# Two layers of channel mixing by 15 products from the third batch element on, their results in banks of two PSUM pools in turn

## The chip, the cores and the metric

The kernel runs on one core of a Trainium2 chip. The metric is the device time of one execution in microseconds. TensorE (PE) multiplies; its weight loads are listed as PEld. VectorE (DVE), ScalarE (ACT) and GpSimd (POOL) do the element work, SyncE (SP) issues most DMAs. Each engine works through its own queue in order. Matmul results stand in PSUM banks, everything else in SBUF.

## The reference

All tensors are float32. The batch has 8 elements b, S = 448 positions, 12 heads of 64, so C = 768 channels.

```python
q_n, k_n = rmsnorm(q, g_q), rmsnorm(k, g_k)
scores = (q_n @ k_n.T) / 8
attn = softmax(scores) ;  x = (attn @ v)            # (8, 448, 768), heads side by side
h = relu(x.T @ w_tok1) @ w_tok2                      # (768 x 448) (448 x 256) (256 x 448)
u = x + h.T
out = u + relu(u @ w_ch1) @ w_ch2                    # 768 -> 1536 -> 768
```

The last line is the channel mixing, two layers of matrix products. The change concerns these.

## The kernel before

**Elements in a pipeline.** PE works in the order in which the program issues its instructions. `middle_items(b)` gives the work of element b as a list of small items: token mixing (`tok1`, `tok2`), then `ch1` (layer 1), then `plain_2` or `ch2` (layer 2). The attention of element b+1 runs in between. For b = 0 and 1 the two lists are merged by their costs (`merge`); from b = 2 on, `place` puts six blocks of attention (`big_step`) before the mixing items number 0, 6, 11, 17, 23 and 31 (`BLOCKS`, line 1209). Blocks are of two kinds in turn. `second_block` makes scores 3 to 6 and the first four value products of a pair of heads. `first_block` makes scores 0, 1 and 2 of the next pair, the last value products of the pair before, and the row sums (`d_ps`). After each block comes its accompanying work: `beside` at once, `between` spread over the items that follow (scaling of q and k, their transposes on DVE, running sums of exponentials `group_sums`, denominators, the roots of `newton` on POOL, loads).

**Layer 1 before.** For every element from b = 1, weights and input are split in two by two quarters, and 7 products stand for 8 (`PRODUCTS`, line 890). The four sums of the input are made in `moving_sums`. An item `ch1(b, mp, i)` is one product for one of three column groups: 6 matmuls of 128x128 by 128x224 into one bank of ps_M. DVE, ACT and POOL add it to the outputs in `hb`. The weights' sums are made from the raw weights on POOL (`sum_items`, lines 242 to 289) and written to DRAM (`ws1`).

**Layer 2 before.** Element 0 (`first_stage`) and element 1 (`plain_2`) are computed plainly. From b = 2 on, `ch2` multiplies 3x2 blocks by 15 products f = 0 to 14 in place of 18, each in two halves x of 4 matmuls. The 15 sums of weights ("forms") are made by `form_items` from `wp2` into `ws2`. The sums of the input blocks are `X_STEPS`, the additions that follow each product `C_STEPS`; the letter v, g or a says which engine does it: DVE, POOL or ACT. An operation on DVE is one of 448 or, in `x_form`, of 896 columns.

**Banks.** PSUM has three pools: ps_S with 4 banks (scores, row sums, transposes), ps_O with 2 (value products), ps_M with 2 (everything else, all mixing products among them). An allocation waits until a bank of its pool has been read.

**Weights.** `load_units` loads units of six 128x128 tiles (384 KB) through SP, up to 7 ahead of their use.

**Timed work.** `later(us, fn)` puts off work by a number of microseconds on a clock that `run` advances by the cost written beside each item. Forms, y's stores and x's way through DRAM (`send_x`, `load_x`) are issued by it:

```python
    def run(items):
        for c, fn in items:
            fn()
            now = clock[0] + c
```

The lines most spoken of: scores L458, their exponentials L462, running sums L499, row sums L511, values L531, denominators L560 and L562, scaling L420, transposes of q and k L435, squares L1394, their reduce L1408, roots L1438 to L1441, transposes of u for the next element L824, tok1 L837 and L844, tok2 L879 and L884, layer 1 L999 to L1030, layer 2 L1048 and L1065 to L1083, input forms L1039, weight forms L320 to L324.

Of the kernel before, what the change touches and what calls it, by code (L numbers as in the profile page):

```python
# [22 lines left out]
NQ = 8  # L23
# [17 lines left out]
    ("ch1", 0): (("v", 6, 1, "+", 3),), ("ch1", 2): (("v", 7, 6, "+", 0),),  # L41
    ("ch1", 3): (("g", 9, 0, "+", 1),), ("ch1", 5): (("v", 8, 7, "+", 2),),
    (0, 1): (("v", 1, 1, "-", 5),), (1, 1): (("v", 6, 9, "-", 5),), (2, 1): (("g", 7, 6, "-", 4),),
    (4, 0): (("v", 4, 7, "+", 2),), (5, 0): (("v", 0, 4, "-", 1),), (7, 1): (("g", 8, 4, "+", 3),)}
# [18 lines left out]
    (("v", (1, 0), (1, 0), "+", "P"),))  # L63

# [19 lines left out]
def whole(ctx, tc, shifted, pre, q, k, v, g_q, g_k, moe_w_tok1, moe_w_tok2, moe_w_ch1, moe_w_ch2, out):  # L84
# [63 lines left out]
    ws1 = dram.tile([KF // 2, NQ, P, KC, 2, P], F32, name="ws1")  # L148
# [17 lines left out]
    def run(items):  # L166
        for c, fn in items:
            fn()
            now = clock[0] + c
# [55 lines left out]
    def slots(j, lo, hi):  # L225

        w, group, m, t = stages[j]
        return ws1[group, lo:hi, :, t, m % 2, :].rearrange("q p n -> p q n")

    def store(j):  # L230

        w, group, m, t = stages[j]
        if group < 3:
            nc.sync.dma_start(out=slots(j, 0, 4), in_=st["stage", j])
            return
        to = wp2[:].rearrange("p (m q t) n -> p q m t n", m=KC, q=4)[:, :, m, t, :]
        nc.sync.dma_start(out=to, in_=st["stage", j])

    def has(group, made):
        return all(j in made for j, s in enumerate(stages) if s[1] == group)  # L240

    def sum_items():


        n = len(stages)

        def make(e, a, q):

            e.tensor_tensor(out=q[:, 6], in0=a[:, 1], in1=a[:, 0], op=ALU.subtract)
            e.tensor_tensor(out=q[:, 4], in0=a[:, 1], in1=a[:, 3], op=ALU.add)  # L250
            e.tensor_tensor(out=q[:, 5], in0=q[:, 6], in1=a[:, 3], op=ALU.add)
            e.tensor_tensor(out=q[:, 7], in0=a[:, 2], in1=q[:, 5], op=ALU.subtract)

        def send(i, e=nc.sync):
            st["summed"].add(i)
            e.dma_start(out=slots(i, 4, 8), in_=eight(st.pop(("sum", i)))[:, 4:8])


        FEW = 8

        def some(i):
            if 2 <= i:
                send(i - 2, nc.gpsimd)
            if i < FEW:
# [722 lines left out]
    def ch1(b, mp, i):  # L987
# [43 lines left out]
        if b > 1 and mp == KF // 2 - 1:  # L1031
            for form in X_STEPS.get(("ch1", i), ()):
                x_form(*form)
# [492 lines left out]
```

## Time and profile before

| | |
|---|---|
| median of 3 runs | 1286.75 us (1286.35 to 1292.13) |
| profiled execution | 1290.15 us, span 1288.2 us |
| PE busy | 1251.4 us (97%) |
| DVE, ACT, POOL busy | 794.4 (62%), 392.2 (30%), 381.7 us (30%) |
| layer 1 (L999) | 1764 matmul records, 352.8 us busy in two groups |
| layer 2 (L1065, L1048) | 1440 records, 277.2 us; 144 wide records, 55.2 us |
| tok1 of b = 0 to 7 begins on PE at | 81.1, 261.8, 424.3, 576.7, 724.5, 872.4, 1020.3, 1165.7 us |

A product of float32 shows as two matmul records. Records of one group overlap in the profile (each lasts about 0.35 us and the next starts after 0.19), so busy time of a group is more than its share of the path where groups alternate. The granted clock of PE (PEclk) is a share of full speed. In the timelines, a line gives the start in us, the length, the engine, the source line, and how often the instruction is repeated; what stands in brackets is the engine's idle time before it and what ended it.

### The profile page before, as it was taken

The numbers are of one execution on the slowest core, as the hardware profiler recorded it, in microseconds if no ns is written. First come the engines' busy times: TensorE is split into PE (matmuls) and PEld (weight loads), VectorE is DVE, ScalarE is ACT, GpSimd is POOL, SyncE is SP. The second block draws the span as 40 slices with busy tenths as digits, with TensorE's granted clock in tenths as the row PEclk, the third lists the DMA queues.
The fourth block names the chain that finished last, engine by engine and source line by source line (L and its number), as shares of the span: only waits on it lengthen the run. The fifth ranks groups of instructions, "written<-read, shape, count | busy, mean of one in ns | idle before, by whom it ended". The sixth has DMA issues, their size and how long they took to land.

```text
span 1288.2 us, 20010 instructions
## 1 busy us (share of the span) xinstructions
PE 1251.4 (97%) x7228; PEld 890.5 (69%) x7228; DVE 794.4 (62%) x1229; ACT 392.2 (30%) x781; POOL 381.7 (30%) x641
## 2 busy tenths in 40 slices
PE   5998999999999999999999999999999999999996
PEld 3444444457744488796778777885787868797996
DVE  6987877846764355855668356765658366544243
ACT  5663333223331144402442043312343033200210
POOL 1303350024996611331223112241122222131231
PEclk9998999999999999999999999999999999999999
DMA  9666494999899876695658767685766864386553
GB/s 209 170 183 184 124 258 115 208 253 250 225 249 239 182 170 165 141 253 116 160 148 184 183 147 179 146 231 115 178 163 149 223 146 135 117 210 156 173 173 82
DMA packets 492864, 228.37 MB, mean 177 GB/s; under 512 B 375508, under 2 KB 453332, under 8 KB 492756
## 3 DMA queue, kind: packets, MB, share of 16 engines
q1 hardware_dynamic: 476178, 213.10, 67.2%
q0 software_dynamic: 3584, 12.06, 3.1%
q10 hardware_dynamic: 12994, 1.84, 0.8%
q8 instruction: 59, 0.97, 0.3%
q14 instruction: 49, 0.40, 0.1%
HBM read 184.26 MB, written 42.66 MB: 176 GB/s over the span
## 4 chain that ended last, share of the span: by engine, by line
PE 84%; DVE 7%; DMA 3%; SPq 2%; issue 1%; ACT 1%; POOL 0%; DVEq 0%; ACTq 0%; POOLq 0%
PE m_ps L999 25%; PE m_ps L1065 21%; PE s_ps L458 9%; PE o_ps L531 9%; PE m_ps L879 5%; PE m_ps L969 5%; PE t_ps L837 2%; PE m_ps L837 2%; PE m_ps L1048 1%; PE m_ps L511 1%; PE d_ps L511 1%; DMA x<-xs 1%; PE t_ps L432 1%; DVE es L499 1%; DVE raw L348 1%
## 5 line engine op out<-in xcount | busy, mean ns | idle before, releaser
L1065 PE MATMUL m_ps<-hb,unit 128*128 128x224 f32 x1440 | 277.2, 354 | 0.0
L1065 PEld LDWEIGHTS m_ps<-hb,unit 128*128 128x128 f32 x1440 | 270.9, 190 | 8.8 <-issue 7.7
L999 PE MATMUL m_ps<-tu,unit 128*128 128x224 f32 x1008 | 201.6, 355 | 1.3 <-ACT r L1009 1.3
L999 PEld LDWEIGHTS m_ps<-tu,unit 128*128 128x128 f32 x1008 | 189.1, 190 | 15.0 <-issue 9.2
L462 ACT ACTIVATE e<-s_ps 128x448 f32<-128x448 f32 x294 | 138.2, 550 | 179.1 <-PE s_ps L458 170.7
L999 PE MATMUL m_ps<-uT,unit 128*128 128x224 f32 x756 | 151.2, 354 | 0.3 <-DVE hb L1005 0.3
L999 PEld LDWEIGHTS m_ps<-uT,unit 128*128 128x128 f32 x756 | 142.2, 190 | 7.4 <-issue 3.9
L458 PE MATMUL s_ps<-qkT 64*64 64x448 f32 x1260 | 143.9, 545 | 0.8 <-ACT x L819 0.8
L531 PE MATMUL o_ps<-e,v 64*64 64x448 f32 x1148 | 129.7, 538 | 0.3 <-ACT uT L568 0.2
L499 DVE TENSOR_TENSOR es<-es,e 128x896 f32<-128x896 f32 x90 | 102.8, 1142 | 14.6 <-ACT e L462 9.3
L1005 DVE TENSOR_TENSOR hb<-m_ps,r 128x448 f32<-128x448 f32 x63 | 39.1, 621 | 109.3 <-POOL r L1005 56.7
L1005 POOL TENSOR_TENSOR hb<-r,r 128x448 f32<-128x448 f32 x21 | 23.9, 1138 | 243.8 <-ACT r L1021 243.8
L458 PEld LDWEIGHTS s_ps<-qkT 64*64 64x64 f32 x1260 | 45.4, 132 | 69.5 <-issue 60.4
L531 PEld LDWEIGHTS o_ps<-e,v 64*64 64x64 f32 x1148 | 45.6, 133 | 62.3 <-issue 58.7
L879 PE MATMUL m_ps<-w_sb,h 128*128 128x448 f32 x192 | 77.3, 555 | 3.6 <-DVE uT L884 3.6
L1006 ACT ACTIVATE hb<-hb 128x448 f32<-128x448 f32 x84 | 48.4, 577 | 100.4 <-DVE hb L1005 78.3
L1438 POOL TENSOR_TENSOR nt<-rs 128x56 f32<-128x56 f32 (+1 forms) x57 | 19.4, 341 | 197.2 <-DVE rs L1430 194.2
L320 POOL TENSOR_TENSOR raw<-raw 128x128 f32<-128x128 f32 x128 | 66.7, 541 | 31.4 <-DMA raw<-wp 26.9
L1080 POOL TENSOR_TENSOR uT<-uT,r 128x448 f32<-128x448 f32 x42 | 51.4, 1238 | 78.5 <-DVE r L1080 46.7
L1005 DVE TENSOR_TENSOR r<-m_ps,r 128x448 f32<-128x448 f32 x42 | 26.1, 622 | 64.1 <-PE m_ps L999 64.1
L884 DVE TENSOR_TENSOR uT<-uT,m_ps 128x448 f32<-128x448 f32 x48 | 29.3, 613 | 59.0 <-PE m_ps L879 59.0
L1408 DVE TENSOR_REDUCE ms<-sq 128x28 f32<-128x896 f32 (+2 forms) x44 | 47.4, 1080 | 27.7 <-ACT sq L1394 24.3
(141 smaller groups left out, 1591.0 us busy)
## 6 DMA issues: line engine op xcount, KB each, us to landing
unit<-ws SPq DMA_DIRECT2D x267, 384.0 KB, 3.9
raw<-in_moe_w_ch_dram SPq DMA_DIRECT2D x72, 256.0 KB, 3.4
v<-in_v_dram SPq DMA_DIRECT2D x96, 112.0 KB, 3.7
xs<-xt SPq DMA_DIRECT2D x56, 168.0 KB, 4.6
out_dram<-turned SPq DMA_DIRECT2D x168, 56.0 KB, 2.0
qk_t<-in_q_dram SPq DMA_DIRECT2D x144, 56.0 KB, 3.4
qk_t<-in_k_dram SPq DMA_DIRECT2D x144, 56.0 KB, 3.6
x<-xs SPq DMA_DIRECT2D x42, 192.0 KB, 3.9
```

What stands on the lines that cost most here:

```text
L320: nc.gpsimd.tensor_tensor(out=at[o], in0=at[x], in1=at[y], op=ALU.add if op == "+" else ALU.subtract)
L458: nc.tensor.matmul(out=pss[i][rows_of(i, a), 0:S], lhsT=qkT[h, 1, k * D:(k + 1) * D], rhs=qkT[h, 0, :], start=True, stop=True)
L462: nc.scalar.activation(out=e[:, i, :], in_=pss[i][:, 0:S], func=AF.Exp)
L499: nc.vector.tensor_tensor(out=es[:], in0=(es if k > 1 else st["e", t, 0])[:], in1=st["e", t, k][:], op=ALU.add)
L531: nc.tensor.matmul(out=st["o", p][a * D:(a + 1) * D, 0:S], lhsT=vt[rows, k * D:(k + 1) * D], rhs=e[rows, :], **kw)
L837: nc.tensor.matmul(out=st["t1", h][jc][:, 0:HC], lhsT=w1_sb[:, c, jc * P:(jc + 1) * P], rhs=st["x", b, h][:, :, c, :], start=start and c = ...
L879: nc.tensor.matmul(out=ps[:, 0:S], lhsT=st["h1", jc][:, cc * P:(cc + 1) * P], rhs=w2_sb[:, jc].rearrange("p c r -> p (c r)"), start=(jc == ...
L969: nc.tensor.matmul(out=ps, lhsT=a[:, o + 2 * half, :], rhs=natural(half * KF + t) if wide else u[:, half * KC + t, :], start=(t == 0 and h ...
L999: nc.tensor.matmul(out=ps[:, j * HS:(j + 1) * HS], lhsT=w[:, t, j, :], rhs=m, start=(t == 0), stop=(t == KC - 1))
L1005: add = lambda e, o, x, y: e.tensor_tensor(out=o, in0=x, in1=y, op=ALU.add)
L1065: nc.tensor.matmul(out=ps[:, x * HS:(x + 1) * HS], lhsT=st["w"][:, tile_at % 6, :], rhs=hb[:, X_SLOT[f], i, :], start=(i == 0), stop=(i == 3))
L1080: e.tensor_tensor(out=get(out), in0=get(x_), in1=get(y), op=ALU.add if op == "+" else ALU.subtract)
```

## The change

Layer 1 takes the scheme that layer 2 had: element 1 is computed plainly (`plain_1`), elements 2 to 7 by 15 products f, each in two column halves o, every one of them an item of 4 matmuls of 128x224 (`ch1(b, f, o)`). The items number 45 before the kept tail in place of 34, and the six blocks stand before items 0, 9, 16, 25, 33 and 40. In layer 1 the half o = 0 goes into a bank of ps_S (`c_ps`) and o = 1 into ps_M. In layer 2 the odd products go into ps_S and the even ones into ps_M.

The input's sums of layer 1 are `X1_STEPS`: three on DVE and one on POOL before the products (`pre_forms`), four on DVE and two on POOL between them. The additions after the products are `C1_STEPS`, done for each o. ReLUs run over 896 columns. Of the four sums of layer 2's input that are made during layer 1, slot 8 goes from DVE to POOL, and all four now stand at f = 12 to 14.

The weights of layer 1 are stored plainly (`wp1`). Both layers' forms are made by one function, `form`: the first at the end of element 0, the other 15 from the beginning of element 1, one for every 15 us of a clock that no longer counts items of a cost up to 1.0 (all that aren't PE's). `sum_items` with its loads and stores goes. The tiles in `wp2` are ordered so that a form is loaded by 3 DMAs in place of 4. The times for x's way through DRAM are set anew for elements 1 and 2. Four mixing items in place of six are kept back after the last block, to stand beside x's transposes (`keep`).

```diff
-NQ = 8
...
 X_STEPS = {
...
+    ("ch1", 12, 1): (("v", 6, 1, "+", 3),), ("ch1", 13, 0): (("v", 7, 6, "+", 0),),
+    ("ch1", 13, 1): (("g", 8, 7, "+", 2),), ("ch1", 14, 0): (("g", 9, 0, "+", 1),),
+    (3, 0): (("v", 1, 1, "-", 5),), (3, 1): (("v", 6, 9, "-", 5),), (4, 1): (("g", 7, 6, "-", 4),),
+    (6, 0): (("v", 4, 7, "+", 2),), (7, 0): (("v", 0, 4, "-", 1),), (8, 0): (("g", 8, 4, "+", 3),)}
...
+NAT = (0, 2, 1)
+X1_SLOT = (0, 1, (2, 0), (0, 0), 2, (2, 1), 4, 3, (1, 1), (1, 0), 2, 4, 0, 1, 5)
+X1_STEPS = {
+    ("pre", 0): (("v", 0, (0, 1), "+", (1, 1)), ("v", 1, 0, "+", (0, 0))),
+    ("pre", 1): (("g", 3, (0, 0), "+", (0, 1)), ("v", 2, 1, "+", (1, 0))),
+    (0, 0): (("v", 4, 3, "-", (2, 1)),), (1, 0): (("v", 5, 4, "-", (2, 0)),), (1, 1): (("v", 0, 5, "+", (1, 0)),),
+    (2, 1): (("g", 1, (0, 1), "-", (2, 1)),), (5, 0): (("v", 2, 0, "-", 1),), (7, 0): (("g", 4, 0, "+", (1, 1)),)}
+
+C1_STEPS = (
...
+    (("a", "B", "P", None, None),),
+    (("v", "A", "A", "+", "P"), ("a", "C", "P", None, None), ("v", "B", "B", "+", "A"),
+     ("g", (0, 0), (0, 0), "+", "B")),
...
+    (("v", (1, 1), "C", "-", "P"), ("v", (2, 1), (2, 1), "+", "P")),
+    (("v", "A", "A", "-", "P"), ("v", (2, 1), (2, 1), "+", "A")),
+    (("v", "A", "A", "+", "P"), ("g", (1, 0), "B", "+", "A"), ("g", (1, 1), (1, 1), "-", "A")),
+    (("v", (1, 0), (1, 0), "+", "P"),))
+RELU = {5: (0, 0), 8: (0, 1), 11: (2, 0), 12: (2, 1), 13: (1, 1), 14: (1, 0)}
...
-            now = clock[0] + c
+            now = clock[0] + (c if c > 1.0 else 0.0)
...
+    FORMS_EVERY = 15.0
+    def form(layer, g):
...
+        def load():
...
+            nc.sync.dma_start(out=flat[:, 0:6 * P].rearrange("p (m n) -> p m n", m=2), in_=rows(0, 2))
+            nc.sync.dma_start(out=flat[:, 6 * P:8 * P], in_=rows(2, 3)[:, 0, 0:2 * P])
+            nc.sync.dma_start(out=last, in_=rows(2, 3)[:, 0, 2 * P:3 * P])
+        def part(i):
...
+            if i == 3:
+                for f, x in W_SINGLE:
+                    nc.gpsimd.tensor_copy(out=at[f], in_=at[x])
+                for lo, t in parts:
+                    nc.gpsimd.dma_start(out=made[:, lo:lo + t.shape[1]], in_=t)
...
+    def later_forms():
+        for n in range(1, 16):
+            at = 2.0 + FORMS_EVERY * (n - 1)
+            load, *parts = form(1 + n // 8, n % 8)
+            later(at, load)
+            for k, fn in enumerate(parts):
+                later(at + 8.0 + 2.5 * k, fn)
...
-            start, step, load = {(1, 1): (2.0, 0.5, 9.0), (2, 1): (2.0, 0.5, 9.0)}.get((b, half), (2.0, 2.0, 12.0))
+            start, step, load = {(1, 1): (0.0, 0.5, 6.0), (2, 1): (0.0, 0.25, 6.0)}.get((b, half), (2.0, 2.0, 12.0))
...
+    def ch1(b, f, o):
         put_off_done()
+        ps = m_tile() if o else s_tile("c_ps")
+        x = X1_SLOT[f]
+        x = x_block(b, *x) if isinstance(x, tuple) else st["tu"][:, x]
+        for t in range(2):
+            for k in range(2):
+                tile_at = f * 8 + o * 4 + t * 2 + k
+                if tile_at % 6 == 0:
+                    st["w"] = next_unit()[:].rearrange("p a b n -> p (a b) n")
+                nc.tensor.matmul(
+                    out=ps[:, t * HS:(t + 1) * HS], lhsT=st["w"][:, tile_at % 6, :], rhs=x[:, k, :],
+                    start=(k == 0), stop=(k == 1))
...
+        for eng, out, a, op, c in C1_STEPS[f]:
+            if op is None:
+                nc.scalar.copy(out=at[out], in_=at[a])
+                continue
+            e = nc.gpsimd if eng == "g" else nc.vector
+            e.tensor_tensor(out=at[out], in0=at[a], in1=at[c], op=ALU.add if op == "+" else ALU.subtract)
+        if o and f in RELU:
...
+            put_off(lambda: nc.scalar.activation(out=t, in_=t, func=AF.Relu))
+        put_off(lambda: x1_forms(b, (f, o)))
+        for step in X_STEPS.get(("ch1", f, o), ()):
+            put_off(lambda step=step: x_form(*step))
+
+    def plain_1(b, m, half):
+        put_off_done()
+        if half == 0:
+            st["m"] = [m_tile() for o in range(2)]
+        u, w = st["uT", b], next_unit()[:].rearrange("p a b n -> p (a b) n")
+        for o in range(2):
+            ps = st["m"][o][:, 0:S]
             for t in range(KC):
                 nc.tensor.matmul(
+                    out=ps, lhsT=w[:, 3 * o + t, :], rhs=u[:, half * KC + t, :],
+                    start=(half == 0 and t == 0), stop=(half == 1 and t == KC - 1))
+            if half:
+                nc.scalar.activation(
+                    out=natural(o * KF + m), in_=ps.rearrange("p (i n) -> p i n", i=2), func=AF.Relu)
...
     def ch2(b, f, x):
         put_off_done()
         if x == 0:
-            st["m"] = m_tile()
+            st["m"] = s_tile("c_ps") if f % 2 else m_tile()
...
-    BLOCKS = (0, 6, 11, 17, 23, 31)
+    BLOCKS = (0, 9, 16, 25, 33, 40)
...
-            tail, keep = (4, 2) if b == 1 else (11, 6)
+            tail, keep = (4, 2) if b == 1 else (11, 4)
```

## The prediction

> **What bounds the kernel now.** I read the page's first part (busy time by engine), then the list of waits by engine, then the timelines of one steady element, and the stretches of time around the one long wait. First the busy times.
>
> ```profile
> PE 1251.4 (97%) x7228; PEld 890.5 (69%) x7228; DVE 794.4 (62%) x1229; ACT 392.2 (30%) x781; POOL 381.7 (30%) x641
> ```
>
> TensorE bounds it: it idles 37 us of 1288.2, some 15 of them at the start and 10 at the end. So the matmul records set the time, and every new wait of TensorE is paid in full. The list of waits of PE has only these two that the change can touch:
>
> ```profile
> PE t_ps L844 <- DMA x<-xs: 2.2, 1, 2.2
> PE m_ps L999 <- ACT r L1009: 1.3, 1, 1.3
> ```
>
> From here I take element b=4, whose span from its first L837 to the next one's is 872.43 - 724.55 = 147.9 us, all of it busy. Its PE timeline around one attention block in the second layer (L1065):
>
> ```profile
> 824.05 12.38 PE L1065 MATMUL m_ps<-hb,unit 128*128 128x224 f32 x64
> 836.35 1.74 PE L458 MATMUL s_ps<-qkT 64*64 64x448 f32 x16
> ...
> 840.91 0.93 PE L458 MATMUL s_ps<-qkT 64*64 64x448 f32 x8
> 841.77 30.82 PE L1065 MATMUL m_ps<-hb,unit 128*128 128x224 f32 x160
> ```
>
> 64 records take 836.35 - 824.05 = 12.3 us, 0.192 each (a product is two records); L999 has the same rate (72 records from 786.33 to 800.15). After the block, at 841.77, mixing goes on at once. Now what the other queues do about that block, on POOL, DVE and ACT:
>
> ```profile
> 815.39 0.28 POOL L1438 TENSOR_TENSOR nt<-rs 128x56 f32<-128x56 f32 x1 [2.09 <-DVE rs L1430]
> ...
> 819.36 0.30 POOL L1441 TENSOR_TENSOR rs<-nt,rs 128x56 f32<-128x56 f32 x1
> ```
> ```profile
> 819.69 3.01 DVE L420 TENSOR_TENSOR qk_t<-qk_t,rs 128x896 f32<-128x896 f32 x2 [1.43 <-POOL rs L1441]
> ...
> 839.31 1.04 DVE L1408 TENSOR_REDUCE ms<-sq 128x28 f32<-128x896 f32 x1
> 841.42 1.08 DVE L1408 TENSOR_REDUCE ms<-sq 128x28 f32<-128x896 f32 x1 [1.06 <-ACT sq L1394]
> ```
> ```profile
> 840.43 0.95 ACT L1394 ACTIVATE sq<-qk_t 128x896 f32<-128x896 f32 x1 [1.16 <-issue]
> 841.88 0.98 ACT L462 ACTIVATE e<-s_ps 128x448 f32<-128x448 f32 x2 [0.49 <-PE s_ps L458]
> ```
>
> The reader should see one chain through in-order queues. POOL's twelve root steps (815.39 to 819.66) release DVE's scaling (819.69, which already waits 1.43 us for them). DVE's queue then leads to the reduce at 839.31. That frees the one `sq` buffer for ACT's second square at 840.43, and the last exponentials of the block stand behind that square on ACT. They start at 841.88, 0.1 us after the block has left PE. Nobody minds today, since mixing takes banks of ps_M and the exponentials empty banks of ps_S. Last, the stretches about the 2.2 us wait at the start of b=2:
>
> ```profile
> 428.00:432.00 4.00, 1.80 (x9) 0.79 (x8) 0.00 (x0) 0.87 (x2) 3.77 (x11) 1.00 1.03 265
> 432.00:434.00 2.00, 2.00 (x7) 0.90 (x5) 0.00 (x0) 0.00 (x0) 1.94 (x4) 0.73 0.70 117
> 434.00:436.00 2.00, 2.00 (x5) 1.09 (x4) 0.65 (x1) 0.00 (x0) 0.22 (x1) 0.50 1.00 252
> 436.00:438.00 2.00, 2.00 (x7) 1.16 (x6) 0.00 (x0) 0.49 (x1) 0.00 (x0) 0.92 0.92 252
> ```
>
> The granted clock falls to 0.73, 0.50 and 0.92 after the wait: 0.54 + 1.0 + 0.16 = 1.7 us more are lost.
>
> **The change part by part.** *Products.* Layer 1 has 21 x 6 x 2 = 252 records an element, 1764 in all, 1764 x 0.192 = 338.7 us. After: 240 records for b=2 to 7 (1440 x 0.192 = 276.5) and, for b=1, 144 records of 448 columns like L1048's (79 in 424.29 - 394.60 = 29.69 us, 0.376 each): 54.1. Sum 330.6, so **-8.1 us**: -13.8 in six elements, +5.7 in b=1. All of it is on the path.
>
> *Stalls that go.* The 1.3 and 0.3 us of L999 are in b=1, whose first layer becomes plain: **-1.6**. Its pairs of ps_M banks are emptied by ACT while 2.26 us of the other bank's products run, against 0.55 us for the activation.
>
> *Load of the other engines, per element.* DVE loses 15 additions (0.62) and the input sums (L900, L901: 3.2 us) and gets 28 + 7 of 0.62: +9.2 us, less 1.1 for a form that goes to POOL, on 86 busy of 148. ACT goes from 10.1 to 12.1 us (12 copies of 0.53, 6 wide ReLUs by the 0.96 of the wide squares). POOL goes from 11.7 to 16.8 (13 of 1.13, one more wide form of 2.09). As averages these are hidden behind PE's 146 us; what counts is where they queue.
>
> *Weights' forms.* The sums of layer 1 go (41.8 us of L249 to L252, with their transfers); eight more forms of 16 x 0.52 + 3 x 0.25 + 2 x 0.94 = 11 us on POOL come. Their spacing of 15 us of PE's items is that of before (eight forms from 317 to 433). From 356 to 395 POOL was busy 36.9 of 39 us and DMA 0.93 with PE never waiting, so I cost it at nothing while b=1 lasts. It now runs 63 us into b=2, beside layer 1's own POOL work. The units of layer 2 are first asked for some 10 us of items after the last form and used some 15 us later, which covers POOL running late by less than that. On SP each form's loads, three for four, now stand before x's loads at the start of b=2, where PE waited 2.2 and lost 1.7; the transfers of x are asked for up to 4.5 us earlier. Bounds -3.9 (the wait goes) to +3.9 (it doubles); I keep it as it is, **0**.
>
> *Banks, first place (A).* At the end of layer 1, after the fourth block, PE goes (12,1), (13,0), (13,1), (14,0), (14,1), each 8 x 0.192 = 1.5 us, then the second layer's first product, which needs the ps_M bank that (13,1) filled. ps_M has two banks. From the end of (12,1), at 1.5, DVE's queue holds: two additions (1.24), two sums of exponentials (2 x 1.1), the form of slot 6 (1.07), (13,0)'s addition (0.62), a denominator's transpose and reciprocal (0.86), the form of slot 7 (1.07), and (13,1)'s addition (0.62): 7.7 us, done at 9.2. PE asks at 7.6. With each operation starting 0.08 before the last one's end, as DVE's rows do, it is 8.5. Wait 0.9 to 1.7 us; I take **1.4** in b=2 to 5 and 1.0 in b=6, which has fewer reduces: **+6.6**. Queued behind on PE is everything.
>
> *Banks, second place (B).* After (13,0)'s addition POOL has four additions (4 x 1.13) and two wide forms (2 x 2.09) before the roots; before there were two additions, done 2.1 us ahead. Counting from the same zero: first pair from 6.6, second from 9.2 to 11.5, forms to 15.7, roots (4.3) and one more addition to 21.1. The fifth block starts on PE at 7.6 + 1.4 + 3 x 1.5 = 13.5. So scaling starts 7.6 us into the block instead of 1.8, and all of DVE's queue with it. From there DVE has two scalings, four qk transposes, four sums, two forms, four additions, three transposes of u: 2 x 1.15 + 4 x 0.62 + 4 x 1.1 + 2 x 1.07 + 4 x 0.62 + 3 x 0.64 = 15.7 us, or 14.4 with the overlap. The next block starts 6.2 + 7 x 1.5 = 16.8 us after the fifth. So the reduce starts 5.2 to 6.5 us into it (2.96 before). Reduce 1.0, square 1.05, exponential 0.55: the first ps_S bank is free at 7.8 to 9.1. Two of the four hold row sums that DVE reads still later. PE leaves the block at 5.42 and the next product, f=5, is odd: it wants ps_S. Wait 2.4 to 3.7 us; if DVE were no later than today, 841.88 + 0.55 - 841.77 = 0.7. I take **2.2**, near the low end of the loaded case because the early wait A gives DVE time, in b=2 to 5: **+8.8**.
>
> *Clock.* A 2.2 us wait cost 1.7 more; waits of 1.3 cost nothing. B stands on that edge: 0 to 4 x 1.7, I take half, **+3.4**.
>
> [...]
>
> *Sum.* -8.1 - 1.6 + 0 + 6.6 + 8.8 + 3.4 = +9.1 us. The profiled execution took 1290.15 (span 1288.2), 3.4 above the median of 1286.75; that is start and end, not the stages above. On the median: 1295.9, so **1296 us**.
>
> **The rivals.** *Banks never bind:* every DVE and POOL row fits, and PE keeps only the shorter products. For it: 86 + 8 busy of 146 on DVE. Against: the two queues counted above. With A and B at nothing: 1286.75 - 9.7 = 1277, or 1273 if b=2's wait goes as well. It ends faster, and decides if A and B together cost under some 3 us, 0.7 an element. *The waits pay back the gain:* A 0.9 and B 0.7 with no clock lost: -9.7 + 4 x 1.6 + 0.6 = -2.7, 1284. *POOL falls behind in b=2 as well:* forms at 11 of every 15 us plus 17 of layer 1 and 10 of roots in 63 us is about 117%; scaling and the last unit loads come late, and each wait of B draws the clock down twice: +9.1 + 3.4 + 6 to 12, 1305 to 1312.
>
> **How the numbers follow.** Forecast (1293 to 1305) 0.47, pay-back 0.24, banks free 0.17, POOL late 0.12. A measurement of this kernel can tell about 0.5% from no change: 6.4 us, so faster is under 1280.3, slower over 1293.2. Faster 0.17, same 0.24, slower 0.59. The range leaves out about one in ten at each end: 1278 (the free case's upper part stays in) to 1309. The extremes of the terms are 1273 and, with A 1.7, B 3.7, every clock loss and b=2's wait doubled, about 1311.
>
> **What would show it.** Right: L999's successor with 1440 records plus 144 wide ones; PE waits on c_ps and m_ps for ACT e and for DVE, some 1.4 and 2.2 us, four times each; DVE's scaling waiting for POOL rs by far more than 1.43; granted clock of 0.5 after the longer waits. Wrong: PE busy throughout b=3 to 5 with elements of 145.6 us (147.9 - 2.3); or a wait at x in place of the banks.

## The result, and the profile after

| | before | after |
|---|---|---|
| median of 4 runs | 1286.55 us | 1318.33 us (1316.91 to 1323.66) |
| profiled execution, span | 1290.15, 1288.2 us | 1318.08, 1316.2 us |

The ratio is 1.0252, 95% interval 1.0204 to 1.0300: slower by 2.5%, 32 us by the medians and 28.0 by the profiled spans. The forecast was 1296 us, range 1278 to 1309: the direction was right, the size was not. Periods of the elements (from one element's first tok1 matmul on PE to the next's, us):

| b | 0 | 1 | 2 | 3 | 4 | 5 | 6 | 7 |
|---|---|---|---|---|---|---|---|---|
| before | 180.6 | 162.5 | 152.4 | 147.9 | 147.9 | 147.9 | 145.3 | 122.5 |
| after | 177.3 | 168.4 | 161.2 | 153.8 | 153.6 | 153.4 | 147.8 | 119.9 |
| change | -3.3 | +5.9 | +8.8 | +5.9 | +5.7 | +5.5 | +2.5 | -2.6 |

The page's first part (busy time by engine), and from the list of waits the lines of PE that are new:

```profile
PE 1262.6 (96%) x7048; PEld 871.8 (66%) x7048; DVE 835.9 (64%) x1280; ACT 403.5 (31%) x775; POOL 469.0 (36%) x727
```
```profile
PE m_ps L1047 <- DVE r L992: 9.4, 5, 2.0
PE c_ps L979 <- ACT e L445: 3.8, 3, 2.8
...
PE c_ps L1047 <- ACT e L445: 2.0, 3, 0.7
...
PE m_ps L979 <- DVE hb L992: 1.7, 1, 1.7
PE s_ps L441 <- DVE r L992: 1.7, 1, 1.7
```

PE has 180 records less and is busy 11.2 us more. The waits listed here are 18.6 us, some 8 of them in b=3 to 5, so they can't carry the +17 us of these elements, where the products alone should have given -7. The rest hides in busy time, and the length of the six attention blocks shows it (first score to next product, b=4): 6.17, 5.42, 6.17, 5.42, 6.17, 5.42 us before; 6.20, 6.00, 7.32, 5.51, 7.28, 6.15 after, the last with a wait of 0.66. PE's timeline of the third block, then what ACT and DVE do meanwhile:

```profile
796.85 2.21 PE L441 MATMUL s_ps<-qkT 64*64 64x448 f32 x14
798.58 0.59 PE L514 MATMUL o_ps<-cv_sb,v 64*64 64x448 f32 x2
798.89 0.54 PE L441 MATMUL s_ps<-qkT 64*64 64x448 f32 x2
...
802.21 2.03 PE L441 MATMUL s_ps<-qkT 64*64 64x448 f32 x14
804.17 1.78 PE L979 MATMUL c_ps<-uT,unit 128*128 128x224 f32 x8
```
```profile
797.87 1.42 ACT L445 ACTIVATE e<-s_ps 128x448 f32<-128x448 f32 x3 [5.39 <-PE s_ps L441]
```
```profile
799.37 0.61 DVE L992 TENSOR_TENSOR hb<-hb,c_ps 128x448 f32<-128x448 f32 x1
```

In the kernel before, such scores are one group of 16 records in 1.74 us: they start in fours (at 780.15, 780.58, 780.96 and 781.33 us), the last by 1.2 us. Here 14 come, and the last two at 798.89, some 0.8 us late: they are the second records of two products that share a bank, whose first records, the last of the 14, begin at 798.46. This bank is free only when ACT has read the block's first score (797.87 + 0.55 = 798.42), since one of the four ps_S banks still holds product (7,0). PE made that from 793.73 to 795.41; DVE reads it at 799.37, 4.0 us later. From 797.65 on the records start in twos (797.65, 798.03, 798.46, 798.89, each lasting 0.54 or 0.59 us), so PE counts as busy and no wait is listed.

The two predicted places, first the wait before layer 2 (PE), then the stretches of time from it on, where the third figure from the right is the granted clock:

```profile
830.47 1.68 PE L979 MATMUL m_ps<-tu,unit 128*128 128x224 f32 x8
834.12 2.41 PE L1047 MATMUL m_ps<-hb,unit 128*128 128x224 f32 x6 [1.97 <-DVE r L992]
```
```profile
832.00:834.00 2.00, 0.15 (x1) 0.00 (x0) 2.00 (x4) 0.00 (x0) 2.00 (x2) 1.00 0.74 196
834.00:836.00 2.00, 1.88 (x6) 1.70 (x7) 1.93 (x6) 0.00 (x0) 2.00 (x3) 0.59 0.32 128
836.00:838.00 2.00, 2.00 (x8) 1.83 (x7) 1.97 (x4) 0.95 (x1) 2.00 (x2) 0.56 0.00 0
```

The granted clock falls to half behind the wait, from 834.36 to 837.77, 3.4 us. Then the chain to the wait behind the sixth block, on DVE, ACT and PE:

```profile
846.05 2.09 DVE L403 TENSOR_TENSOR qk_t<-qk_t,rs 128x896 f32<-128x896 f32 x2 [6.35 <-POOL rs L1421]
```
```profile
862.10 1.04 DVE L1388 TENSOR_REDUCE ms<-sq 128x28 f32<-128x896 f32 x1
```
```profile
863.22 0.95 ACT L1374 ACTIVATE sq<-qk_t 128x896 f32<-128x896 f32 x1 [1.66 <-DVE ms L1388]
864.17 0.98 ACT L445 ACTIVATE e<-s_ps 128x448 f32<-128x448 f32 x2
```
```profile
864.76 1.40 PE L1047 MATMUL c_ps<-hb,unit 128*128 128x224 f32 x6 [0.66 <-ACT e L445]
```

So b=4 is accounted for: products -2.3, blocks +3.0, wait before layer 2 +2.1, half a clock for 3.4 us +1.7, wait behind the sixth block +0.7, a short wait at (13,0) +0.5: +5.7 of +5.7. Here waits between products are counted from one record's start to the next one's. The listed idle begins at a record's end, 0.35 us behind its start, where the next would have started after 0.19; so such a wait costs 0.16 us more than is listed (2.13 for 1.97, 0.51 for 0.35).

In b=2 ACT's squares also wait for q and k, which they never do there in the kernel before, and the exponentials stand behind them:

```profile
471.45 0.95 ACT L1374 ACTIVATE sq<-qk_t 128x896 f32<-128x896 f32 x1 [3.28 <-DMA qk_t<-in_k_dram]
504.98 0.95 ACT L1374 ACTIVATE sq<-qk_t 128x896 f32<-128x896 f32 x1 [3.14 <-DMA qk_t<-in_q_dram]
516.97 0.95 ACT L1374 ACTIVATE sq<-qk_t 128x896 f32<-128x896 f32 x1 [4.76 <-DMA qk_t<-in_k_dram]
```

### The profile page after: what moved, and what is told of

It reads as the page before. It is cut to its first block, busy times and chain, and to the rows that moved or that the text cites. A ratio compares the mean times of both kernels' runs of the same rounds, so it can differ in the third digit from the quotient of the medians.

```text
span 1316.2 us, 19628 instructions
## 1 busy us (share of the span) xinstructions
PE 1262.6 (96%) x7048; PEld 871.8 (66%) x7048; DVE 835.9 (64%) x1280; ACT 403.5 (31%) x775; POOL 469.0 (36%) x727
## 4 chain that ended last, share of the span: by engine, by line
PE 77%; DVE 10%; DMA 4%; SPq 3%; POOL 2%; issue 2%; ACT 2%; DVEq 0%; ACTq 0%; POOLq 0%
PE m_ps L1047 12%; PE c_ps L1047 10%; PE s_ps L441 8%; PE c_ps L979 8%; PE m_ps L979 7%; PE o_ps L514 7%; PE m_ps L862 5%; PE m_ps L1010 4%; PE m_ps L935 4%; PE m_ps L1030 4%; PE t_ps L820 2%; PE m_ps L820 2%; DVE es L482 2%; DMA qk_t<-in_k_dram 2%; DVE hb L1021 1%
## 5 line engine op out<-in xcount | busy, mean ns | idle before, releaser
L1047 PE MATMUL m_ps<-hb,unit 128*128 128x224 f32 x768 | 160.4, 364 | 9.4 <-DVE r L992 9.4
L1047 PEld LDWEIGHTS m_ps<-hb,unit 128*128 128x128 f32 x768 | 150.3, 197 | 12.5 <-DVE r L992 11.1
L295 POOL TENSOR_TENSOR raw<-raw 128x128 f32<-128x128 f32 x256 | 135.2, 549 | 45.8 <-DMA out_dram<-turned 25.5
L1047 PE MATMUL c_ps<-hb,unit 128*128 128x224 f32 x672 | 135.8, 354 | 2.6 <-ACT e L445 2.0
L1047 PEld LDWEIGHTS c_ps<-hb,unit 128*128 128x128 f32 x672 | 126.3, 190 | 9.9 <-ACT e L445 4.3
L979 PE MATMUL c_ps<-tu,unit 128*128 128x224 f32 x480 | 101.5, 354 | 3.9 <-ACT e L445 3.8
L979 PE MATMUL m_ps<-tu,unit 128*128 128x224 f32 x480 | 102.1, 356 | 1.7 <-DVE hb L992 1.7
L979 PEld LDWEIGHTS m_ps<-tu,unit 128*128 128x128 f32 x480 | 89.7, 190 | 9.9 <-issue 5.6
L979 PEld LDWEIGHTS c_ps<-tu,unit 128*128 128x128 f32 x480 | 90.1, 190 | 9.2 <-ACT e L445 7.6
L403 DVE TENSOR_TENSOR qk_t<-qk_t,rs 128x896 f32<-128x896 f32 (+1 forms) x42 | 55.6, 1361 | 43.5 <-POOL rs L1421 43.5
```

The costliest lines, as they stand in the source:

```text
L295: nc.gpsimd.tensor_tensor(out=at[o], in0=at[x], in1=at[y], op=ALU.add if op == "+" else ALU.subtract)
L403: nc.vector.tensor_tensor(out=x, in0=x, in1=r.unsqueeze(2).to_broadcast(list(x.shape)), op=ALU.mult)
L979: nc.tensor.matmul(out=ps[:, t * HS:(t + 1) * HS], lhsT=st["w"][:, tile_at % 6, :], rhs=x[:, k, :], start=(k == 0), stop=(k == 1))
L1047: nc.tensor.matmul(out=ps[:, x * HS:(x + 1) * HS], lhsT=st["w"][:, tile_at % 6, :], rhs=hb[:, X_SLOT[f], i, :], start=(i == 0), stop=(i == 3))
```

## The experiments

All start from the changed kernel, except where one names the kernel before. "Period" is that of b=4, unless said otherwise; ratios are to the kernel before on the same chip. A period comes from one profiled execution, and that can lie off the median: 5.3 us above it in the run with less work for DVE, 4.4 us below it in the one with less for POOL.

### Which banks: all products in ps_M

```diff
-        ps = m_tile() if o else s_tile("c_ps")
+        ps = m_tile()
...
-            st["m"] = s_tile("c_ps") if f % 2 else m_tile()
+            st["m"] = m_tile()
```

> All products of both layers get their bank from ps_M, as before the change; everything else is the changed kernel. Theory (score tiles wait for banks): in b=3 to 5 the changed kernel loses about 2.9 us an element because blocks of attention start while an unread product still holds one of the four ps_S banks (7.32 and 7.28 us for blocks that took 6.18, 6.01 for one of 5.42), and 1.2 us more in waits on c_ps. These blocks then return to about 6.2 and 5.4 us and the waits on c_ps vanish: -4.1 us an element. Against that DVE reads (6,0) and (6,1) some 2 us later than a pool of two banks allows, so waits on m_ps of DVE grow by 2 to 5 us an element, and the clock may fall after them. Total 1300 to 1330 us. Rival (the queues are late, the pools don't matter): blocks stay at 7.3 and 6.0 us, and the total only grows by the new waits on m_ps, 1325 to 1345.

1324.3 us, ratio 1.0289 (1.0264 to 1.0314), period 154.1. The six blocks are 6.18, 5.42, 6.17, 5.42, 6.17 and 5.42 again, 34.8 us in all. PE's third block, then PE's longest lines of waits:

```profile
799.33 1.74 PE L441 MATMUL s_ps<-qkT 64*64 64x448 f32 x16
...
803.89 1.68 PE L441 MATMUL s_ps<-qkT 64*64 64x448 f32 x16
```
```profile
PE m_ps L979 <- DVE hb L992: 19.3, 15, 3.3
PE m_ps L979 <- DVE r L992: 15.5, 10, 2.5
```

So the longer blocks are products in ps_S. But ps_M alone costs 8.1 us of waits an element, about what blocks, waits and clock cost in the changed kernel (8.0): DVE reads too late for two banks.

### Layer 2 alone, undone and done alone

Undone (second line pair of the diff above only):

> The changed kernel with layer 2's products all in ps_M again; layer 1 keeps its turns. Theory (score tiles wait for banks): the block before item 33 no longer starts with a ps_S bank held by a half-made product and returns from 7.28 to 6.2 us, the wait of 0.7 us behind the sixth block goes; the other blocks stay at 6.0, 7.3 and 5.5. The wait before layer 2's first product stays near 1.9 us with its 1.7 us of clock, and its successors on ps_M follow in 3 us steps: -1.8 us an element in b=2 to 6, 1309 us (1306 to 1313). Rival (ps_M gives the time back, as it did when both layers used it): one or more waits on m_ps of DVE in layer 2 of 1 us or more, 1316 to 1322.

1314.8 us, ratio 1.0199 (1.0174 to 1.0224), period 152.3. As expected the fifth block is 6.17 us and the wait behind the sixth goes. As the rival expected, ps_M takes 1.3 and 0.9 us back in layer 2 (1.14 and 0.72 of it listed as idle). The rest of the gain is the clock, of which more below.

Done alone, in the kernel before:

```diff
-            st["m"] = m_tile()
+            st["m"] = s_tile("c_ps") if f % 2 else m_tile()
```

> The kernel before, with one part of the change alone: layer 2's odd products in ps_S. There every block starts behind a product in ps_M and with ps_S read. Theory: block lengths stay at 6.17 and 5.42 us, and PE waits only for the first exponential behind the fifth and the sixth block (products f = 1 and 5), 0.3 to 0.7 us each: 147.9 becomes 148.5 to 149.3 us an element, total 1290 to 1293. Rival 1 (the turn alone carries the loss): blocks longer by 1 us, waits of 2 us, 1300 or more. Rival 2 (exponentials are done in time): 1286 to 1288.

1290.1 us, ratio 1.0023 (1.0009 to 1.0038), period 148.3 against 147.9. All blocks keep their length but the wait behind the sixth appears:

```profile
840.37 1.97 PE L1065 MATMUL c_ps<-hb,unit 128*128 128x224 f32 x9 [0.63 <-ACT e L462]
```

It is as long as in the changed kernel, though POOL's roots are on time here. Behind the fifth block I had expected a wait too; there is none.

### The clock by itself: fill the wait with work

```diff
-        for t in range(2):
-            for k in range(2):
+        again = 1 + ((f, o) == (14, 1))
+        for t, k in [(t, k) for _ in range(again) for t in range(2) for k in range(2)]:
+            if True:
```

> The four matmuls of layer 1's last product half (14,1) are issued twice, in all of b=2 to 7: 1.5 us more work, result unchanged, right where TensorE waits 1.9 us for ps_M in b=2 to 5. Theory (a wait and its clock are two prices): the work takes the place of the wait, which shrinks to about 0.4 us, and the 3.4 us at half clock behind it go, so b=2 to 5 get 1.7 us shorter each although they do more; b=6 (wait 1.4) stays as it is, b=7 gets 1.5 longer: total about 1318 - 6.8 + 1.5 = 1313. Rival (the clock falls whatever stands there, or the wait moves on with the extra work): +1.5 us an element, 1326.

1317.4 us, ratio 1.0240 (1.0215 to 1.0266); periods of b=3 to 5: 152.4, 151.4, 151.5, so 1.4 to 2.2 us shorter with 1.5 us more work. From b=2 on the granted clock never falls. The stretches where the changed kernel had 0.59 and 0.56:

```profile
834.00:836.00 2.00, 2.00 (x12) 2.00 (x11) 1.97 (x4) 0.51 (x1) 2.00 (x3) 1.00 0.40 157
836.00:838.00 2.00, 2.00 (x13) 1.53 (x16) 1.93 (x5) 1.17 (x2) 2.00 (x2) 1.00 0.70 195
```

The theory holds for the mechanism; the total gains 1 us rather than 5, since b=7 pays 2.0 and b=2 gains only 0.5.

### Who is late: less work for DVE, less for POOL

```diff
-    ("ch1", 12, 1): (("v", 6, 1, "+", 3),), ("ch1", 13, 0): (("v", 7, 6, "+", 0),),
+    ("ch1", 12, 1): (("a", 6, 1, "+", 3),), ("ch1", 13, 0): (("a", 7, 0, "+", 0),),
...
-    (("v", "A", "A", "+", "P"), ("a", "C", "P", None, None), ("v", "B", "B", "+", "A"),
+    (("v", "A", "A", "+", "P"), ("a", "C", "P", None, None),
...
-    (("v", "B", "B", "+", "P"), ("v", "C", "C", "-", "B")),
+    (("v", "B", "B", "+", "P"),),
...
-    (("v", "A", "A", "-", "P"), ("v", (2, 1), (2, 1), "+", "A")),
+    (("v", "A", "A", "-", "P"),),
```

> The changed kernel with work taken off DVE around the products, about 5.9 us an element: left out are the additions B + A (f=4), C - B (f=6) and (2,1) + A (f=12) of layer 1, and layer 2's input sums of slots 6 and 7, which ACT fills with a copy of one operand. Banks and blocks are as in the changed kernel. Theory (DVE reads products about 4 us late, and whichever bank they hold, someone waits): the third block, which waited for the bank of (7,0), returns from 7.32 to about 6.2 to 6.6 us, the wait of 1.9 us before layer 2 goes, its clock too; the fifth (7.28: a half-made product holds a bank) and the second (6.0) change little. 153.6 becomes 148 to 149.5 us an element, total 1292 to 1302. Rival (POOL sets the pace, DVE only passes its lateness on): 153 us, 1315 to 1318.

1295.5 us, ratio 1.0054 (1.0035 to 1.0073); periods of b=3 and 5: 148.2 and 148.1 (b=4 150.8, with a wait of 2.0 us behind the sixth block and a fall of the clock to 0.50 at 854 us). The third block is 6.20 us, the wait before layer 2 is gone, the second and fifth blocks are unchanged, as the theory said. It had not foreseen that the wait behind the sixth block grows, to 1.0 to 1.1 us in b=3 and 5 as well. DVE's reading of (7,0) and PE's third block:

```profile
789.06 0.61 DVE L992 TENSOR_TENSOR hb<-hb,c_ps 128x448 f32<-128x448 f32 x1
```
```profile
786.25 1.68 PE L979 MATMUL c_ps<-tu,unit 128*128 128x224 f32 x8
787.77 1.68 PE L979 MATMUL m_ps<-tu,unit 128*128 128x224 f32 x8
789.37 1.74 PE L441 MATMUL s_ps<-qkT 64*64 64x448 f32 x16
```

DVE reads (7,0) 1.1 us after it is made in place of 4.0, before the block's last scores need its bank, and the 16 records are one group again.

```diff
-    ("ch1", 13, 1): (("g", 8, 7, "+", 2),), ("ch1", 14, 0): (("g", 9, 0, "+", 1),),
...
-    (("v", "A", "A", "+", "P"), ("g", (1, 0), "B", "+", "A"), ("g", (1, 1), (1, 1), "-", "A")),
+    (("v", "A", "A", "+", "P"),),
```

> The changed kernel with work taken off POOL alone: left out are the four additions behind (13,0) and (13,1) in layer 1 and the wide input sums of slots 8 and 9, 8.7 us an element, all of it ahead of the roots on POOL's queue. The recorded prediction's step for the second wait: roots, scaling and with them the reduce and the exponentials come late because of these six operations; then the wait of 0.7 us behind the sixth block goes or shrinks, and scaling starts within 2 us of the block's start. Theory now (DVE had slack there, and that wait comes from the bank itself): scaling no longer waits 6.35 us, but the wait behind the sixth block stays at 0.7 us, the one before layer 2 at 1.9, the blocks at 7.3: 153 to 153.7 us an element, b=2 2 to 4 us shorter, 1311 to 1316. Rival (POOL is the cause of most of the loss): 150 or less, under 1303.

1311.0 us, ratio 1.0181 (1.0159 to 1.0203), period 150.8: between the two. Scaling still waits 2.77 us where it waited 6.35, blocks and the wait of 0.7 are unchanged, so POOL's lateness is not what that wait is made of. But the wait before layer 2 fell to 1.4 and the clock stayed up (1.00 in b=4 from 820 to 842 us), which I had not expected. Part of it is this: DVE's sum of slot 7, in the changed kernel beside POOL's additions, 1.40 us, and here without them, 1.03:

```profile
832.13 1.40 DVE L1021 TENSOR_TENSOR hb<-hb 128x896 f32<-128x896 f32 x1
```
```profile
825.63 1.03 DVE L1020 TENSOR_TENSOR hb<-hb 128x896 f32<-128x896 f32 x1
```

### Can banks and places alone remove it?

Five kernels kept all work and moved banks or single steps.

```diff
-    BLOCKS = (0, 9, 16, 25, 33, 40)
+    BLOCKS = (0, 8, 16, 24, 32, 40)
```

> The six blocks stand before items 0, 8, 16, 24, 32 and 40 in place of 0, 9, 16, 25, 33 and 40, so that none starts right behind a product in ps_S, or between the two halves of one. Theory (score tiles wait for banks): the block at item 8 returns from 6.0 to 5.4 us and the one at item 32 from 7.3 to 6.2, the one at item 16 stays near 7.3: -1.7 us an element in b=2 to 6, 1309 to 1313 us; the wait before layer 2's first product stays at 1 to 2 us. Rival (the blocks are longer since DVE and ACT are late, wherever they stand): same block lengths, 1316 to 1321.

1332.4 us, ratio 1.0354 (1.0331 to 1.0378), period 154.0, b=2 169.8. The block at item 32 is 6.18 us as expected, and the one at item 8 5.5 plus a wait of 0.6. I had overlooked that items 8, 16 and 24 themselves take ps_S: the product behind the block now waits for an exponential, up to 5.2 us in b=2.

```diff
+IN_M = "MMSSMSSMM" "MMSSSMM" "MMSSMSSMM" "MMSSS"
...
-        ps = m_tile() if o else s_tile("c_ps")
+        ps = m_tile() if IN_M[2 * f + o] == "M" else s_tile("c_ps")
...
-            st["m"] = s_tile("c_ps") if f % 2 else m_tile()
+            st["m"] = s_tile("c_ps") if f == 2 else m_tile()
...
-    BLOCKS = (0, 9, 16, 25, 33, 40)
+    BLOCKS = (0, 9, 16, 25, 32, 40)
```

> The changed kernel with other banks: the two product halves ahead of a block and the two behind it take ps_M, those in the middle of a stretch ps_S (layer 2: only f = 2 in ps_S), and the fifth block stands before item 32 in place of 33. So no block starts while a fresh product holds a ps_S bank, no product needs ps_S right behind a block, and layer 2's first product needs the bank of (12,1), not that of (13,1). Theory (banks at the blocks' edges are the loss): blocks return to 34.8 us an element (38.5 in the changed kernel, 34.8 before), the waits on m_ps before layer 2 and their clock go: steady elements 146 to 147.5 us, below the 147.9 of before; b=2 155 to 158; total 1283 to 1292. Rival (DVE and POOL are too late for any choice of banks): waits of 1 to 2 us reappear on other products, steady elements 151 to 154, 1305 to 1318.

1317.4 us, ratio 1.0215 (1.0196 to 1.0234), period 154.1: the rival's figures. The blocks take 36.3 to 38.0 us in b=3 to 5, not 34.8 (the third still 7.32). The wait before layer 2 is gone, and this has come in its place, a product behind row sums that DVE has not turned yet:

```profile
PE c_ps L980 <- DVE dt L544: 9.3, 5, 2.9
```

Next only slot 7's sum was moved, behind (14,1)'s addition:

```diff
-    ("ch1", 12, 1): (("v", 6, 1, "+", 3),), ("ch1", 13, 0): (("v", 7, 6, "+", 0),),
-    ("ch1", 13, 1): (("g", 8, 7, "+", 2),), ("ch1", 14, 0): (("g", 9, 0, "+", 1),),
+    ("ch1", 12, 1): (("v", 6, 1, "+", 3),), ("ch1", 13, 1): (("g", 9, 0, "+", 1),),
+    ("ch1", 14, 1): (("v", 7, 6, "+", 0), ("g", 8, 7, "+", 2)),
```

> The changed kernel with one operation of DVE moved: layer 2's input sum of slot 7 (1.07 us) is issued behind (14,1)'s addition in place of ahead of (13,1)'s; slot 8, which needs it, follows on POOL behind slot 9. Theory (the wait before layer 2 is DVE's queue ahead of (13,1)'s addition, term by term): the wait falls from 1.92 to about 0.85 us; if a wait that short leaves the clock alone, as the 1.45 us in b=6 did, 153.6 becomes about 150.8 us an element, total 1307 to 1311; with the clock as it is 152.5, 1313. Rival (DVE's queue is limited elsewhere): wait and total within 0.3 us and 3 us of the changed kernel.

1337.6 us, ratio 1.0382 (1.0358 to 1.0405), period 156.8. The wait before layer 2 falls to 0.60 us, further than the theory said, but f = 1 needs slot 7 and now waits 3.9 us for it, with 6.8 us at half clock from 846 us on. Then that move with other banks and places:

```diff
+IN_M = "MMSSMSMM" "MMSSMSSMM" "MMSSMSMM" "MMSSM"
...
+            st["m"] = s_tile("c_ps") if f in (2, 3, 6) else m_tile()
...
+    BLOCKS = (0, 8, 17, 25, 33, 41)
```

> Banks chosen by how late DVE reads, together with the move of slot 7: blocks before items 0, 8, 17, 25, 33 and 41; products next to a block in ps_M, and in the middle of a stretch so that a bank is asked for again no sooner than two products after the one that filled it; layer 2 in ps_M but for f = 2, 3 and 6. In the earlier choice of banks three products in ps_S stood in a row behind a first block, whose row sums still held two of its four banks (3.0 us of waits for L544). Theory (every wait is DVE's lag against the distance of a bank's next use): blocks 34.8 to 36 us an element, waits under 1 us, steady elements 146 to 148.5 us, total 1284 to 1296. Rival (DVE's and POOL's bursts exceed any choice of banks): a steady element of 150 or more, 1303 to 1318.

1342.4 us, ratio 1.0421 (1.0400 to 1.0442), period 156.9. And without the move of slot 7, f = 8 in ps_S as well:

> As the second choice of banks and block places, but slot 7 stands where the changed kernel has it (on DVE ahead of (13,1)'s addition), and layer 2's f = 8 takes ps_S too, so that f = 9 needs the bank of f = 5. Theory (every wait is DVE's lag against the distance of a bank's next use): the wait of 5.3 us for slot 7 and that of 2.2 us in layer 2 go, blocks stay at 35.1 us, steady elements 145.6 to 148.5 us against 147.9 in the kernel before; b=2 still longer than 158 by POOL's forms; total 1288 to 1300. Rival (the burst of DVE work at the end of layer 1 must be paid somewhere): a wait of 1 to 2 us before layer 2 or in the fifth block, steady elements 150 or more, over 1303.

1334.5 us, ratio 1.0382 (1.0349 to 1.0415), period 156.7. In both, layer 1 has become free of loss (63.9 us from its first to its last record; 65.6 in the changed kernel), and the blocks of b=4 add up to 35.1 and 35.5 us. All of it, and more, comes back in layer 2 (67.8 us for 60.8), where PE now waits for DVE and for a sum of POOL's:

```profile
PE m_ps L1048 <- DVE hb L993: 15.4, 5, 3.8
...
PE m_ps L1048 <- POOL hb L1022: 13.0, 4, 3.3
```

None of these choices got the steady elements below 150 us, as the rivals of the three choices of banks had said; their totals were 1317.4, 1342.4 and 1334.5 us. The rivals of the other two runs were wrong: in the first a block did get its length back, in the second the wait did fall, and both kernels lost more elsewhere.

### The extra loss in b=2

```diff
-    FORMS_EVERY = 15.0
+    FORMS_EVERY = 11.0
```

> One weight form for every 11 us of the clock in place of 15, so that the fifteenth is asked for some 56 us earlier, near the end of b=1. Theory (b=2's extra loss of 3 us comes from POOL, where forms stand ahead of roots and of layer 1's additions): b=2's period falls from 161.2 to about 155 to 157 us, b=1 stays within 2 us, b=3 to 5 stay at 153.6; total 1311 to 1316. Rival (b=2 loses by its own DVE work or by the transfers of x): b=2 stays at 160 to 162, and b=1 grows by the denser transfers: 1318 to 1325.

1346.6 us, ratio 1.0469 (1.0441 to 1.0498). b=2's layer 1 falls from 73.1 to 65.1 us, but b=1 grows to 193.2 and b=2 begins with 11 us of waiting for x, so that its period is 167.1. SP's queue, then PE's:

```profile
SPq L289 <- DMA ws<-raw: 80.7, 10, 10.2
```
```profile
PE t_ps L827 <- DMA x<-xs: 12.5, 2, 11.0
```

Loads of forms wait at the head of SP's queue for raw buffers that earlier forms are still being stored from; everything behind them is late. With 13.0 and the first choice of banks:

> The same choice of banks, and one weight form for every 13 us in place of 15. 11 us were too close: forms' loads then stood on SP's queue waiting for raw buffers, and v and x came late. Theory: at 13 us POOL (11.7 us a form and some 1.3 us of roots) still keeps up, b=1 grows by less than 1 us, and b=2 gets 2 to 4 us shorter than with 15, since fewer forms stand ahead of its roots and additions: 1280 to 1288. Rival (SP's queue fills up again): loads of forms wait for raw buffers in b=1, x or v comes late there, b=1 or b=2 grows by 3 us or more: 1288 to 1300.

1324.3 us, ratio 1.0281 (1.0253 to 1.0309); b=1 grows to 183.5, b=2 falls to 159.0 from that choice's 163.3. The mechanism is the rival's; both ranges of time had taken for granted that the choice of banks would win.

```diff
-                nc.gpsimd.tensor_tensor(
-                    out=at[o], in0=at[x], in1=at[y], op=ALU.add if op == "+" else ALU.subtract)
+                nc.gpsimd.tensor_copy(out=at[o], in_=at[x])
```

> The changed kernel with the 16 additions of each weight form on POOL replaced by 16 copies of one operand (about 0.25 us for 0.52): the sums are left out, loads, stores and spacing are kept. A form takes POOL some 6 us in place of 11.7. Theory (b=2's loss over b=3 to 5, 3 us of 8.8 by the periods and 7.5 us of 73.1 in its layer 1, is POOL's forms ahead of roots and additions): b=2 falls from 161.2 to 154 to 156 us, b=3 to 5 stay at 153.6, b=1 within 1 us: 1311 to 1314. Rival (DMA or DVE cause it): b=2 stays above 159.5, 1316 to 1319.

1313.1 us, ratio 1.0191 (1.0163 to 1.0219). b=2 stays at 160.7 and ACT's squares there wait for q and k as before (5.2 us the longest): less time of POOL's in the forms alone doesn't shorten it. That is less than clearing POOL. Two waits of 1.7 us behind DVE are gone, and the fourth block takes 6.1 us in place of 8.0; but the second takes 10.1 in place of 6.0, since a late square holds the exponentials and a score waits 2.0 us for ACT, and the clock falls there once more than in the changed kernel (0.50 from 470 to 472 us as well as at 528). The total lies in the theory's range by luck: in b=3 to 5, after the last form, the clock never falls here (1.00 throughout), and these elements are 4.0 us shorter together.

```diff
-        [(1.0, fn) for fn in form(1, 0)]
+        [(1.0, fn) for g in (0, 1) for fn in form(1, g)]
...
-        for n in range(1, 16):
-            at = 2.0 + FORMS_EVERY * (n - 1)
+        for n in range(2, 16):
+            at = 2.0 + FORMS_EVERY * (n - 2)
```

> As pick_3, with two weight forms at the end of b=0 in place of one and all others 15 us earlier, so that the last is asked for 48 us into b=2 in place of 63. Theory (forms stand ahead of b=2's roots and additions on POOL): b=2 gets 2 to 5 us shorter than in pick_3, b=0 and b=1 stay within 1.5 us. Rival (raw buffers are short at the end of b=0): loads for b=1 stand behind the second form's loads on SP, b=0 or b=1 grows by 2 us or more.

1340.8 us, ratio 1.0421 (1.0399 to 1.0443). b=1 and b=2 grow by 3.3 and 5.1 us over the third choice of banks; b=2 begins with a wait of 6.3 us before tok2. The rival was right. Last, q's and k's loads moved ahead on SP:

```diff
-        between = [item(turn_qk, n + 1, 1), item(turn_qk, n + 1, 0)] + loads(n + 2) if more else []
-        between += [item(group_sums, t, k) for k in (5, 6)] + loads(n + 3)
+        between = [item(turn_qk, n + 1, 1), item(turn_qk, n + 1, 0)] + fours(loads(n + 2)) if more else []
+        between += fours(loads(n + 3)) + [item(group_sums, t, k) for k in (5, 6)]
```

> The changed kernel with the loads of q and k behind a second block moved: they follow the transposes four at a time, both pairs ahead of the last two running sums, so that SP issues the last of them some 4 us earlier. Theory (late transfers of q and k hold ACT's squares, and with them the exponentials and DVE's reduce): the squares of the block before item 25 no longer wait, DVE's reduce comes some 3 us earlier, the wait before layer 2 falls from 1.9 to about 0.9 us and its clock with it where the wait becomes too short: 153.6 becomes 150.5 to 152.5 us; in b=2 the wait of 2.8 us for an exponential behind a late square shrinks, 161.2 becomes 156 to 159: total 1304 to 1312. Rival (q and k come late since DVE frees their buffers late, so earlier places in SP's queue change nothing): squares wait as before, total 1316 to 1320.

1313.9 us, ratio 1.0199 (1.0167 to 1.0230), 2 us above the expected range. b=2 falls by 2.9 us to 158.3, period 151.8. ACT's squares in b=2 now:

```profile
470.95 0.95 ACT L1377 ACTIVATE sq<-qk_t 128x896 f32<-128x896 f32 x1 [0.84 <-DMA qk_t<-in_k_dram]
506.20 0.95 ACT L1377 ACTIVATE sq<-qk_t 128x896 f32<-128x896 f32 x1 [2.88 <-DMA qk_t<-in_q_dram]
513.59 0.94 ACT L1377 ACTIVATE sq<-qk_t 128x896 f32<-128x896 f32 x1
```

Late transfers of q and k are thus a part of b=2's loss. In b=4 DVE's reduce before layer 2 no longer idles for 4.7 us but 1.0; the wait there only falls from 1.97 to 1.81 us. The wait at (13,0) goes, the fourth block grows from 5.5 to 6.4 us, and the gain of the steady elements is the clock, which stays up (1.00 in every 2 us of b=3 to 5).

No kernel here beats the one before.

## Why the prediction was wrong

By its steps, against the profiled spans (+28.0 us; predicted +9.1):

- *Products, stalls of L999.* Right: b=7, where nothing else happens, is 2.6 us shorter (2.3 were put), b=1 5.9 longer (5.7, less 1.6 of stalls, which went; a wait of 1.6 us for x came in b=1).
- *Weights' forms, 0 with bounds of -3.9 to +3.9.* The lower bound came for x in b=2: wait and half clock are both gone. What was not seen is how late b=2 gets otherwise: waits of 1.7 and 2.8 us at products, blocks longer by 5.8 (one with a wait of 1.7 us in it). Late loads of q and k are a part of it.
- *First place, A.* Right in place and mechanism, 2.1 us for 1.4 (b=6: 1.7 for 1.0). Of what the count of DVE's queue left out, two rows show a part: slot 7's sum takes 1.40 us, not 1.07, and the reduce starts late since its square waits for k. With the reduce 3.7 us less idle the stretch from (12,1) to layer 2 was 0.8 us shorter, but most of that was the wait at (13,0); the wait before layer 2 itself fell by 0.16.
- *Second place, B.* 2.2 was put, 0.7 measured in four elements, -6.1 in all. The chain exists (scaling waits 6.35 us for POOL), but scaling starts 5.5 us into the fifth block, not 7.6, and the block itself lasts 1.1 longer, so the reduce comes 3.5 us into the next block, not 5.2 to 6.5. The value was the lower bound that the text named, "if DVE were no later than today", as the turn in the kernel before shows with 0.63.
- *Clock.* +3.4 was put at B, and A was taken to cost nothing. It is the other way: B costs none, A costs 1.7 in each of b=2 to 5, +6.8.
- *The step that failed.* "Nobody minds today, since mixing takes banks of ps_M and the exponentials empty banks of ps_S": from this the prediction asked only when a product waits for a score's bank. It left out the other direction, a score waiting for a product's bank in a block. That term was missing in the sum and is the largest: +3.0 us in each of b=3 to 5, 3.1 in b=6, 5.8 in b=2, some 18 us. With all products in ps_M, every block has its old length again.

The terms again: 9.1 + 18 (blocks) + 5 (b=2's other waits) + 3.6 (A) + 3.4 (clock) + 1.6 (at (13,0)) + 1.6 (x in b=1) - 6.1 (B) - 3.9 (x in b=2) - 3.3 (b=0, where a wait of 2.8 us cost 6.8 us at half clock in the profiled execution of before, and one of 2.4 us cost none after) = 29, 1 more than measured. The prediction had put those 3.4 us of the profiled execution down to start and end. That B was put 6.1 too high, and that x's wait in b=2 went, hid a part of what the sum left out.

Of the rivals, "POOL falls behind in b=2 as well" came nearest in time (1305 to 1312), and its reason was not confirmed: with the forms' additions made cheaper on POOL, b=2 as a whole stayed where it was. Under all of it is what taking work off DVE showed: behind a first block DVE reads products about 4 us after PE has made them ((7,0) is done at 795.41 and read at 799.37, (13,1) at 829.13 and 833.46). That DVE is busy 64% on average told nothing of that. How far b=2's remainder is the load on the DMA engines (mean share 0.98 from 445 to 475 us, 0.69 in the same stretch before), how far late buffers of q and k, and how far POOL, stays open.

## What to carry to other kernels

When a pool of banks gets a new user, count both directions: the new user waiting for the old one's banks, and the old one waiting for the new one's; small products that run four at a time can lose time without any idle being listed (here a block of 7.32 us for 6.17), so compare lengths of the same block. If the reader of the banks is late by more than a bank's time to its next use, another choice of banks may only move the wait, as the three choices here did (1317.4, 1342.4 and 1334.5 us for 1318.33); first take work from the reader in that stretch. A load that waits for a buffer can hold up what stands behind it on SP's queue: with a form for every 11 us SP waited up to 10.2 us, and PE 11.0 us for x.

## What the runs showed of the hardware

**Half clock followed cells of 3.41 us with much idle time in them.** In the changed kernel the four stretches at half clock (0.50) between b=2 and b=5 begin at 527.2, 680.8, 834.4 and 988.0 and last 3.41 us each; they lie 153.6 us apart, 45 times 3.4133. In one run with many falls (the second choice of banks), eleven stretches at half clock begin at times that all leave 1.9 us, within 0.1, on division by 3.4133 us. Ten last 3.4 us, one 6.8. I laid cells of that length over four runs (changed, second choice, first choice, layer 2 undone), placed by each run's own falls, and added up PE's idle time in each cell. Of 21 full-speed cells with 1.88 us or more of idle, 20 are followed by a cell at half clock. Of the 38 with 0.9 to 1.83 us, none is. In the kernel before, the cells with 1.86 us (from 429.51) and 2.07 us (from 108.65) are followed by one, the cell with 0.92 us (from 337.35) isn't. So in these runs the same wait was cheap or dear by where it fell: 1.97 us inside one cell (830.95 to 834.36 in the changed kernel) was followed by 3.41 us at 0.50, which costs 1.7 more. With layer 2 undone, a wait of the same length across a cell's edge (0.56 us of idle in one cell, 1.41 in the next) cost nothing:

```profile
834.15 1.59 PE L1047 MATMUL m_ps<-hb,unit 128*128 128x224 f32 x7 [1.97 <-DVE r L992]
```
```profile
834.00:836.00 2.00, 1.85 (x10) 1.85 (x11) 1.93 (x6) 0.00 (x0) 2.00 (x3) 1.00 0.36 141
```

In the changed kernel an element came out at 153.4 to 153.8 us, about 45 cells (153.6), so that b=2 to 5 hit nearly the same place of the grid. Why the clock falls, no run here shows.

**DVE was slower beside POOL.** The same 128x896 sum took 1.40 us while POOL added (changed kernel, 832.13), and 1.03 without (less work for POOL, 825.63, with POOL idle from 822 to 828). In the changed kernel's whole trace the 132 operations of DVE on two inputs of this shape with no addition of POOL of 128x128 or more beside them took 1.04 to 1.09 us; the 39 that ran beside one for nine tenths of their time or more took 1.45 on average, up to 2.02. Why, no run here shows.
